# Last outputs formed in one VectorE operation, and the first key weights loaded in two quarters

## Chip, cores and metric

One core of a Trainium2 chip. The metric is the device time of one execution in microseconds (us), the median over runs. The span that a profile shows is some 1.8 us shorter than the device time of the same execution.

## Reference

A linear-attention block and a token-mixing MLP, both with a residual, in bf16:

```python
x = A_x                                            # [1, 2048, 1024]
h  = x + A(layernorm(x), wqkv, wo)                 # linear attention, phi(t) = elu(t) + 1
h2 = h + B(layernorm(h), w1, b1, w2, b2)           # mixer over the sequence, F = 3584
# B: u = gelu(h^T w1 + b1);  y = (u w2 + b2)^T
```

What matters for the change: at the start the first tiles of x are normalised, transposed and multiplied by the key columns of `wqkv`. At the end the last outputs are a matrix product plus `b2` plus the residual `h`.

## The kernel before

The head. `wkv` holds key and value weights; `hk` is half of the 8 row blocks. SP is the SyncE queue.

```python
xs = {0: load_x(0, True)}              # x tile 0, one half on SP's queue, one on ACT's
xs[1] = load_x(1)                      # SP
pin(nc.scalar.dma_start(wkv[:, 0:hk, 0:CW], wqkv_v[:, 0:hk, D:D + CW]))      # 512 KB, ACT's queue
nc.sync.dma_start(wkv[:, hk:ND, 0:CW], wqkv_v[:, hk:ND, D:D + CW])           # 512 KB, SP's queue
# ... cut: ACT's table load, x tile 2, more key weights, x tiles 3 to 5 ...
k_parts(0, 0, range(0, 6))             # PE: first six key matmuls, need row blocks 0 to 5
# ... cut ...
transpose_in(2)                        # PE transposes x tile 2, ACT copies it out of PSUM
ln_stats(3); stats(3)                  # fourth x tile: DVE statistics, ACT log and exp (rstd)
phi_dve((0, 0))
w_sums(kmov, slice(0, 1))              # DVE, a sum of weights, 1.2 us
norm_halves(3)                         # DVE normalises the fourth tile
# ... cut ...
transpose_in(3)                        # PE transposes it
```

The last quad. A quad is four 128-row output tiles, made by products with sums of weight blocks; there are four quads. For the last one the residual is fetched into SBUF (`self.hr`), so its outputs are stored plainly and not accumulated in DRAM.

```python
def out(self, sh, dh, a, b, op):
    # ... cut: choose ot, a piece of a dead weight buffer ...
    op(ot[:, a:b], b2_sb[:, i:i + 1])                                    # ACT (or DVE): PSUM + bias
    to = o_dram[i * P:(i + 1) * P, dh * CW + a:dh * CW + b]
    if (sh, dh) in self.hr:
        dve.tensor_tensor(ot[:, a:b], ot[:, a:b], self.hr[sh, dh][:, a:b], ALU.add)
        nc.sync.dma_start(to, ot[:, a:b])
    else:
        nc.gpsimd.dma_start(to, ot[:, a:b], accum_op=ALU.add)

def evac(self, sh, dh, ps, a=0, b=CW):
    self.out(sh, dh, a, b, lambda ot, bias: nc.scalar.activation(
        ot, ps[:, a:b], ACT.Identity, bias=bias, scale=1.0))
```

The very last product is cut into 384 and 128 columns, so that the first piece can leave while PE works on the second. In the middle, `load_w2(p, 0)` brings the next quad's even rows of `w2` (896 KB for each of two products) as soon as their buffer is free, and DVE's sums (`is`) read them.

## Time and profile before

Before: 559.9 us, median of three runs (559.51 to 560.59). The prediction below shows the lines of its profile. Four distances read from its trace:

| distance | before, us | how to read it |
|---|---|---|
| x tile 4 to transposes | 3.73 | from the first statistics of the fourth x tile (13.28) to PE's first transpose of it (17.01) |
| PE middle | 513.10 | from PE's 200th weight load to its 3380th, of 3387: nearly all work after the head |
| store lag | 1.42 | from the end of the 384 columns' matmuls (554.65) to the issue of the last store (556.07) |
| closing | 3.63 | from the end of the last matmul (555.04) to the end of the span (558.67) |

Matmul ends are modelled in such a trace, but in the same way in every kernel here.

### The profile page before, as it was taken

To read this page: it belongs to the slowest core of one execution; us is meant where nothing else is said; L and a number is where in the kernel's file an instruction comes from. 1 tells how busy PE (TensorE), PEld (TensorE's weight loads), DVE (VectorE), ACT (ScalarE), POOL (GpSimd) and SP (SyncE) were. 2 spreads that over 40 slices of the span, in tenths; PEclk is the share of its full clock that TensorE was granted. 3 is DMA by queue.
4 is the path that set the end of the run, shared out by engine and by line. 5 is a ranking of instruction groups with operands and counts; after the bars stand their busy time and mean duration, and the time that the engine had idled before them with its cause. 6 is when DMAs were issued, how large, how long until landed. Compare 5 with 4: busy or idle time off the path is not lost.

```text
span 558.7 us, 8921 instructions
## 1 busy us (share of the span) xinstructions
PE 550.3 (98%) x3370; PEld 320.7 (57%) x3387; DVE 442.7 (79%) x858; ACT 291.7 (52%) x619; POOL 26.2 (5%) x36
## 2 busy tenths in 40 slices
PE   7999999999999999999999999999999999999997
PEld 3444446645444444456766766666444667767665
DVE  6898888764579688889989889897996878749746
ACT  4747778676777877645455565464310312413312
POOL 1000000000000000000000000000003103103111
PEclk9999999999999999999999999999999999999999
DMA  9933332201956971202240431413769659849434
GB/s 306 298 76 76 76 76 39 39 0 47 340 151 176 325 208 75 76 0 74 80 151 0 151 122 31 150 38 96 197 209 237 190 127 244 212 133 238 93 106 74
DMA packets 83915, 74.51 MB, mean 133 GB/s; under 512 B 15634, under 2 KB 76320, under 8 KB 83872
## 3 DMA queue, kind: packets, MB, share of 16 engines
q1 hardware_dynamic: 79104, 69.61, 41.9%
q0 software_dynamic: 4096, 3.68, 4.8%
q10 hardware_dynamic: 672, 0.66, 0.4%
q8 instruction: 26, 0.43, 0.3%
q14 instruction: 17, 0.14, 0.1%
HBM read 59.12 MB, written 11.67 MB: 127 GB/s over the span
## 4 chain that ended last, share of the span: by engine, by line
PE 93%; DMA 2%; DVE 2%; ACT 1%; SPq 1%; issue 1%; DVEq 0%; ACTq 0%
PE psI L234 25%; PE psC L234 16%; PE acc_t L234 14%; PE psB L234 8%; PE psC L965 4%; PE psB L965 4%; PE psA L965 4%; PE psB L346 2%; PE psA L346 2%; PE acc_t L1295 2%; PE psE L965 2%; PE psC L346 2%; PE acc_t L887 2%; DMA x_sb<-in_A_x_dram 1%; PE psA L234 1%; PE kvps L916 1%
## 5 line engine op out<-in xcount | busy, mean ns | idle before, releaser
L234 PEld LDWEIGHTS <-is 128*128 128x128 f16 x736 | 71.8, 98 | 31.2 <-DVE hi L234 0.4
L234 PEld LDWEIGHTS <-sa 128*128 128x128 f16 x606 | 59.3, 98 | 27.1
L234 PEld LDWEIGHTS <-wq 128*128 128x128 bf16 (+1 forms) x496 | 48.4, 98 | 28.2 <-issue 1.0
L234 PE MATMUL acc_t<-wo_sb,pqT 128*128 128x512 f16 x256 | 55.6, 379 | 0.0
L492 POOL DMA_DIRECT2D out_dram<-wq x28 | 24.3, 927 | 520.3 <-DVE sa L338 401.3
L234 PEld LDWEIGHTS <-pqT 128*128 128x128 bf16 x256 | 24.9, 98 | 30.5 <-issue 0.6
L234 DVE TENSOR_TENSOR t<-psI,t 128x256 f32<-128x256 f32 (+1 forms) x45 | 20.8, 475 | 22.2 <-PE psI L234 20.9
L194 DVE TENSOR_SCALAR e_sb<-e_sb 128x512 bf16<-128x512 bf16 x64 | 18.4, 288 | 21.9 <-ACT e_sb L189 21.8
L234 PE MATMUL psC<-gs,wq 128*128 128x512 f16 x140 | 34.1, 379 | 0.0
L965 PEld LDWEIGHTS <-xs 128*128 128x128 f16 x208 | 20.1, 98 | 22.5 <-DVE xs L954 1.1
L234 PE MATMUL psC<-hT,sa 128*128 128x512 f16 x112 | 31.2, 379 | 0.0
L234 PE MATMUL psI<-hi,is 128*128 128x256 f16 x200 | 30.0, 273 | 0.0
L234 PE MATMUL psB<-hT,sa 128*128 128x512 f16 x112 | 29.7, 379 | 0.0
L234 PE MATMUL acc_t<-xnT,wq_sb 128*128 128x512 bf16 x125 | 29.3, 379 | 0.3
L189 ACT ACTIVATE e_sb<-acc_t 128x512 bf16<-128x512 f32 x32 | 19.1, 598 | 18.6 <-PE acc_t L1295 10.0
L234 DVE BATCH_NORM_STATS2 hst<-acc_t 128x6 f32<-128x512 f32 x32 | 21.4, 692 | 9.0 <-ACT h_bf L234 8.9
L965 PE MATMUL psA<-wkv,xnT 128*128 128x512 bf16 x98 | 26.2, 379 | 0.3
L965 PEld LDWEIGHTS <-xnT 128*128 128x128 bf16 x156 | 15.3, 98 | 18.0 <-issue 0.2
L234 PE MATMUL psC<-hT,wq 128*128 128x512 f16 x96 | 24.6, 379 | 0.0
L234 ACT CAST h_bf<-acc_t 128x512 bf16<-128x512 f32 x32 | 18.4, 581 | 11.9 <-PE acc_t L234 11.8
L234 DVE TENSOR_TENSOR e<-psI,es 128x256 f32<-128x256 f32 x20 | 8.5, 425 | 19.9 <-PE psI L234 17.8
L234 ACT COPY psI<-psI 128x256 f32<-128x256 f32 x50 | 18.0, 360 | 11.6 <-PE psI L234 9.7
(244 smaller groups left out, 1133.9 us busy)
## 6 DMA issues: line engine op xcount, KB each, us to landing
wq<-in_B_w_dram SPq DMA_DIRECT2D x14, 1024.0 KB, 7.9
wq<-in_B_w_dram SPq DMA_DIRECT2D x12, 896.0 KB, 7.4
gs<-parked SPq DMA_DIRECT2D x9, 896.0 KB, 4.7
shared_sb<-rd_dram SPq DMA_DIRECT2D x32, 128.0 KB, 3.8
out_dram<-h_bf SPq DMA_DIRECT2D x16, 256.0 KB, 2.0
x_sb<-in_A_x_dram SPq DMA_DIRECT2D x15, 256.0 KB, 3.0
w2o<-in_B_w_dram SPq DMA_DIRECT2D x4, 896.0 KB, 10.9
out_dram<-wq POOLq DMA_DIRECT2D x28, 128.0 KB, 5.0
```

Of the source, the lines that this page charges most:

```text
L189: pin(nc.scalar.activation(e_sb[:], src, ACT.Exp))
L194: pin(nc.vector.tensor_scalar(e_sb[:], e_sb[:], 1.0, PHI_EPS, ALU.min, ALU.add))
L234: return (lambda *a, **kw: pin(op(*a, **kw))) if self.always or getattr(Held, self.key) else op
L346: pe.matmul(ps[:, cols], lhsT=lhs[:, k, :], rhs=mv(k)[:, cols], start=(start and k == 0), stop=(k == self.nk - 1), skip_group_check=True,)
L492: nc.gpsimd.dma_start(to, ot[:, a:b], accum_op=ALU.add)
L887: mm = nc.tensor.matmul(pp[:, 0:CW], lhsT=xnT[:, kt, i * P:(i + 1) * P], rhs=wkv[:, kt, c * CW:(c + 1) * CW], start=(kt == 0), stop=(kt == ...
L916: pin(nc.tensor.matmul(kv_ps[b][:, sl, :], lhsT=pks[i % NPK][:, j * P:(j + 1) * P], rhs=vaugs[i % NVA][:, j, :], start=False, stop=(i == N ...
L965: pin(nc.tensor.matmul(ps[:], lhsT=lhs[:, k, :], rhs=rhs[:, k, :], start=(start and k == 0), stop=(k == hk2 - 1), skip_group_check=True,))
L1295: nc.tensor.matmul(qp[:, 0:SW], lhsT=wq_sb[:, kt, j * P:(j + 1) * P], rhs=xnT[:, kt, u * SW:(u + 1) * SW], start=(kt == 0), stop=(kt == ND ...
```

## The change

The intent: take ACT out of the last outputs, so that one DVE operation adds bias and residual to the PSUM value, and let the first key matmuls start when half of their weights are there. The diff, cut to its core:

```diff
-        def out(self, sh, dh, a, b, op):
+        def out(self, sh, dh, a, b, op, src):
             if (sh, dh) in self.hr:
-                ot = odd[self.p - 2][:, r:r + 2, :].rearrange("p a b -> p (a b)")
+                ot = odd[self.p - 2][:, r:r + 2, :].rearrange("p a b -> p (a b)")[:, a:b]
+                dve.scalar_tensor_tensor(ot, src, bias, self.hr[sh, dh][:, a:b], ALU.add, ALU.add)
+                hd.dma_start(to, ot)
             else:
-            op(ot[:, a:b], b2_sb[:, i:i + 1])
-            if (sh, dh) in self.hr:
-                dve.tensor_tensor(ot[:, a:b], ot[:, a:b], self.hr[sh, dh][:, a:b], ALU.add)
-                nc.sync.dma_start(to, ot[:, a:b])
-            else:
+                op(ot[:, a:b], bias)
                 nc.gpsimd.dma_start(to, ot[:, a:b], accum_op=ALU.add)
 ...
-            pin(nc.scalar.dma_start(wkv[:, 0:hk, 0:CW], wqkv_v[:, 0:hk, D:D + CW]))
+            for k in (0, hk // 2):
+                pin(nc.scalar.dma_start(wkv[:, k:k + hk // 2, 0:CW], wqkv_v[:, k:k + hk // 2, D:D + CW]))
```

(`evac` and `evac_shared` pass `src`, the PSUM columns or None for the sum in SBUF.)

More of the change, by code (lines that the diff above doesn't have):

```diff
@@ L476, in fetch @@
             self.hr[sh, dh] = t
-        def out(self, sh, dh, a, b, op):
+        def out(self, sh, dh, a, b, op, src):
             i = 2 * self.p + sh
+            to = o_dram[i * P:(i + 1) * P, dh * CW + a:dh * CW + b]
+            bias = b2_sb[:, i:i + 1]
             if (sh, dh) in self.hr:
                 r = 6 * dh + 2 + 2 * (a > 0)
-                ot = odd[self.p - 2][:, r:r + 2, :].rearrange("p a b -> p (a b)")
+                ot = odd[self.p - 2][:, r:r + 2, :].rearrange("p a b -> p (a b)")[:, a:b]
+                dve.scalar_tensor_tensor(ot, src, bias, self.hr[sh, dh][:, a:b], ALU.add, ALU.add)
+                hd.dma_start(to, ot)
             else:
@@ L485, in out @@
                 ots.append(ot)
-            op(ot[:, a:b], b2_sb[:, i:i + 1])
-            to = o_dram[i * P:(i + 1) * P, dh * CW + a:dh * CW + b]
-            if (sh, dh) in self.hr:
-                dve.tensor_tensor(ot[:, a:b], ot[:, a:b], self.hr[sh, dh][:, a:b], ALU.add)
-                nc.sync.dma_start(to, ot[:, a:b])
-            else:
+                op(ot[:, a:b], bias)
                 nc.gpsimd.dma_start(to, ot[:, a:b], accum_op=ALU.add)
@@ L495, in evac @@
             self.out(sh, dh, a, b, lambda ot, bias: nc.scalar.activation(
-                ot, ps[:, a:b], ACT.Identity, bias=bias, scale=1.0))
+                ot, ps[:, a:b], ACT.Identity, bias=bias, scale=1.0), ps[:, a:b])
         def evac_shared(self, sh, ps):
             self.out(sh, 1, 0, CW, lambda ot, bias: dve.scalar_tensor_tensor(
-                ot, ps[:], bias, self.e[:], ALU.add, ALU.add))
+                ot, ps[:], bias, self.e[:], ALU.add, ALU.add), None)
         def done(self):
```

## The prediction

> **What bounds the kernel now.** I read the page first: TensorE (PE) is busy for 550.3 of 558.7 us. Then the busy time by stage. The columns are the stretch, its length, then busy us and instructions of PE, weight load, VectorE (DVE), ScalarE (ACT) and POOL, then granted clock, DMA share and GB/s:
>
> ```profile
> 0.00:17.00 17.00, 13.53 (x70) 5.79 (x71) 11.40 (x43) 9.24 (x23) 1.89 (x8) 1.00 0.94 315
> 17.00:60.00 43.00, 42.49 (x223) 20.41 (x228) 37.84 (x82) 26.78 (x56) 0.00 (x0) 1.00 0.51 131
> 60.00:500.00 440.00, 439.21 (x2683) 256.38 (x2694) 352.60 (x664) 238.85 (x505) 13.90 (x16) 1.00 0.44 126
> 500.00:552.00 52.00, 52.00 (x377) 36.50 (x376) 38.80 (x65) 14.18 (x32) 10.45 (x12) 1.00 0.59 144
> 554.70:558.70 4.00, 0.34 (x7) 0.17 (x3) 0.88 (x3) 0.82 (x2) 0.00 (x0) 1.00 0.32 98
> ```
>
> From 17 us to 554.7 us PE has almost no hole (42.49 of 43.00, 439.21 of 440.00, 52.00 of 52.00) at full clock. So only the head, 17 us with 3.5 us of PE idle, and the tail, about 3.6 us after the last matmul, can give anything. The change touches exactly these two. What it can win is a few us at most, under 1% of 560.
>
> The head on PE, in order of time (start, length, what, idle before it and who ended it):
>
> ```profile
> 8.56 1.45 PE L887 MATMUL acc_t<-wkv,xnT 128*128 128x512 bf16 x6 [1.75 <-DMA wkv<-in_A_wqkv_dram]
> ...
> 14.63 1.89 PE L887 MATMUL acc_t<-wkv,xnT 128*128 128x512 bf16 x8
> 17.01 0.72 PE L1176 MATMUL tp<-ident,xn 128*128 128x128 bf16 x8 [0.49 <-DVE xn L866]
> ```
>
> The first line is the wait that the split is meant to shorten. The last is a second, later hole, which DVE ends. To see what sets that one I read the chain of waits in the head (start, length, what):
>
> ```profile
> 5.14 8.11 DMA x_sb<-in_A_x_dram
> ...
> 13.28 1.30 DVE st L856 x2
> ...
> 15.41 1.22 DVE shared_sb L939
> 16.63 0.34 DVE xn L866
> ...
> 17.01 0.72 PE tp L1176 x8
> ```
>
> The chain does not go through the key weights at all. It goes through the load of the fourth x tile, which lands at 13.26, then through DVE without a pause (statistics, a weight sum, the normalisation), then PE. Whatever PE does before 17.01, it waits there.
>
> The tail, from the same view:
>
> ```profile
> 552.00 2.66 PE psC L234 x14
> ...
> 554.69 0.59 ACT wq L495
> ...
> 555.30 0.36 DVE wq L234
> 555.66 0.14 DVEq L1833
> ```
>
> The last output columns are made by two operations in a row: ACT reads PSUM and adds the bias, DVE adds the residual in bf16. Then SyncE (SP) issues the stores. Its last two, in the timeline:
>
> ```profile
> 555.69 0.33 SPq L490 DMA_DIRECT2D out_dram<-wq  x1
> 556.07 0.43 SPq L490 DMA_DIRECT2D out_dram<-wq  x1
> ```
>
> The last landed at 557.63, and the end comes 1.04 us later, at 558.67.
>
> **What the Trainium skill says.** "Perfetto Trace Analysis", section Optimizing Scalar/DVE Operations: each operation has a fixed cost besides its elements (about 125 ns on DVE from PSUM) and some work can sit on either engine. The trace agrees on a fixed part: ACT takes 580 ns for 384 columns and still 359 for 128.
> "PSUM — Partial Sum Buffer", section Specifications: a VectorE instruction may take at most one tensor input from PSUM. The new operation has one (psC); bias and residual are in SBUF. The trace already holds this form, with one PSUM input and a per-partition bias, at 742 ns.
> "VectorE: DVE Perf Modes", section The perf-mode tier table: a two-tensor operation runs at two elements per cycle on bf16 in SBUF and at one with PSUM or fp32. The trace agrees: 425 ns for the old bf16 add of 512 columns, 742 for the form that reads PSUM. So the merged operation is slower than the DVE part that it replaces, and is a gain only because the ACT part before it goes.
> "DMA: Bandwidth & Descriptors", section Issuing engines are not separate DMA queues: transfers run on the same 16 DMA engines, whoever issues them. The head moves 315 GB/s at a DMA share of 0.94, so cutting a load in two adds no bandwidth; it can only let some of it be used sooner.
>
> **Part one, the final outputs.** Five outputs of the last quad change: two from a sum in SBUF, three from PSUM (512, 384 and 128 columns). Five ACT operations go, and five bf16 adds on DVE become five three-input operations. The built program confirms it: ACT loses five rows, DVE keeps its number and order, PE and the stores keep their order. The durations of what goes and what comes:
>
> ```profile
> L234 DVE SCALAR_TENSOR_TENSOR wq<-psC,b_sb,e 128x512 bf16<-128x512 f32 x6 | 4.5, 742 | 0.0
> ...
> L495 ACT ACTIVATE wq<-psC,b_sb 128x384 bf16<-128x384 f32 x1 | 0.6, 580 | 0.1
> L495 ACT ACTIVATE wq<-psC,b_sb 128x128 bf16<-128x128 f32 x1 | 0.4, 359 | 0.0
> ```
>
> Per column the three-input form costs about 1.04 ns (fp32 adds: 691 for 512, 420 for 256, so 271/256 = 1.06). Hence about 742 - 128 x 1.04 = 609 ns for 384 columns and 742 - 384 x 1.04 = 343 ns for 128. Now step through DVE; where two operations are both ready, the trace starts the second about 0.085 us before the first's end.
> Output 1: its sum is ready at 551.75; the operation runs 551.78 to 552.52 and is off the path.
> Output 2: sum ready at 553.30; 553.33 to 554.07.
> Output 3 (PSUM, 512): ready about 553.55, but DVE is taken; 553.99 to 554.73.
> Output 4 (PSUM, 384): its last matmul ends at 554.65, so as ACT did before it starts at 554.69, just as DVE comes free; to 555.30. Before, ACT and then DVE were done with it at 555.66.
> Output 5 (PSUM, 128): matmul done at 555.04; 555.21 to 555.56. Before: 555.80.
> The two last stores are 0.38 us apart in the trace (556.07 - 555.69): SP's own spacing, 0.33 issue plus 0.05. The fourth store follows its DVE operation by 0.03: 555.33. The fifth could start at 555.58 but waits for SP: 555.71 instead of 556.07. Gain 0.36 us on the path, set by the 384-column piece (580 + 359 and two hand-overs become 609 and one), not by the smallest. From issue to landing (1.56 us) and the closing 1.04 us do not change. There is perhaps 0.06 us more: SP ends with a fixed list of completion checks 0.06 apart, and as the split shifts the assignment of completion semaphores by one, the last store's stands one place nearer the end of the list.
> Sum of part one: 0.36 to 0.42 us.
>
> **Part two, the key weights.** The 512 KB on ACT's queue was issued at 1.18 and took 7.2 us: 8.4, and the first matmul began at 8.56. The x half before it on that queue landed at 0.74 + 2.7 = 3.4. If the weights arrive evenly between, the first quarter lands near (3.4 + 8.4)/2 = 5.9, my estimate. The first matmul then waits for ACT's copies of the transposed x (start 6.63, two in 0.65), so it moves to about 7.1. The third still needs the second quarter at 8.4, or up to 8.9 (1.67 + 7.2) if that now shares with SP's half. So two matmuls of 0.215 us move into the hole, and the group ends 0 to 0.43 us earlier than 10.0. All this lies before 17.01, where PE waits anyway: the second hole grows from 0.49 us to as much as 0.9. Bytes ahead of the fourth x tile are the same, so 13.26 stays. Worth on the path: 0. ACT's extra issue (0.45 us) delays its table load to about 2.1 to 3.4; its first operation is at 4.87, so that is free.
>
> **Sum.** 559.9 - 0.4 + 0 = 559.5 us.
>
> **Rivals.** (a) The split pays in full, because the fourth x tile is not what bounds the head. Then 0.43 us more: 559.1. For it: the wait removed is the longest of PE, 1.75. Against: the chain and the 0.49 hole at 17.01.
> (b) DVE becomes the bound of the tail: outputs 2 to 4 run on it back to back from 553.33, and at 50 ns more each than I reckon, the 384 piece starts late. That costs 0.1 to 0.15 of the 0.36: 559.7. For it: my margin at 554.69 is about 0.04 us.
> (c) The end does not follow the stores, because their landing is set by the DMA engines or by another queue. Then 559.9. Against: the last landing followed its issue by 1.56 and the DMA share is 0.32.
> (d) Two loads on ACT's queue push SP's loads, the fourth x tile among them, back by their issue time. Then up to 0.4 us later: 559.9 to 560.0. For it: every extra issue costs 0.4 to 0.5 us. Against: it is on ACT's sequencer, and SP's fourth tile is issued 8 us before it lands.
>
> **Range and chances.** The three runs before spread over 1.1 us, more than the gain, and the head hangs on when a DMA lands. So 558.9 to 560.2. No rival comes near 2% (11 us): chance of within 2% 0.99, the rest for a surprise either way.
>
> **What would show it.** Right: five ACT operations on the last outputs gone, DVE three-input operations of about 742, 609 and 343 ns, last store issued about 0.67 us after the last matmul instead of 1.03; first key matmul near 7.1, a hole before the third, and a hole ended by DVE at 17.0 that is larger than 0.49. Wrong: PE leaving that hole at another time than 17.0 (part two then acts through the x load), the 384 piece starting later than its matmul, or a new hole on PE between 17 and 554 us.

## The result, and the profile after

After: 560.12 us median of six runs (558.96 to 562.50), beside 559.70 for the kernel before in the same rounds. The ratio is 1.0008, with a 95% interval of 0.9985 to 1.0031: the same. A ratio here is the mean time of one kernel's runs over that of the other's of the same rounds, so it is not quite the ratio of the medians quoted. Executions over 1.5% slower than the fastest of the same kernel are left out of the means.

The tail moved as intended. The tail part of the chain of waits of the changed kernel (start, length, what):

```profile
552.33 2.31 PE psC L234 x12
554.64 0.43 issue
555.07 0.62 DVE wq L234
555.69 0.26 DVEq L1833
```

ACT is gone from it: PE, one DVE operation, then the closing. (The "issue" of 0.43 is read further down.) The groups of DVE instructions in the last 8 us have the mean ns of one as the number after the comma:

```profile
L234 DVE SCALAR_TENSOR_TENSOR wq<-psC,b_sb,wq 128x512 bf16<-128x512 f32 x1 | 0.7, 743 | 0.0
L234 DVE SCALAR_TENSOR_TENSOR wq<-psC,b_sb,wq 128x384 bf16<-128x384 f32 x1 | 0.6, 618 | 0.4 <-issue 0.4
...
L234 DVE SCALAR_TENSOR_TENSOR wq<-psC,b_sb,wq 128x128 bf16<-128x128 f32 x1 | 0.3, 342 | 0.0
```

The two last stores in the timeline, now one row of two issues, 555.72 and 556.10 in the trace:

```profile
555.72 0.81 SPq L234 DMA_DIRECT2D out_dram<-wq  x2
```

The last matmul ends at 555.37 here, so the last store leaves 0.73 us after it (before 556.07 - 555.04 = 1.03). The last stage by engine (same columns as in the prediction) shows ACT empty and DVE with two operations instead of three; the first line is the head:

```profile
0.00:17.00 17.00, 13.55 (x72) 5.72 (x73) 11.45 (x43) 9.13 (x23) 1.89 (x8) 1.00 0.91 307
...
554.70:558.70 4.00, 0.67 (x9) 0.43 (x7) 0.88 (x2) 0.00 (x0) 0.00 (x0) 0.87 0.31 98
```

In the head PE is busy for 13.55 us, as before (13.53). Its timeline says why the split brought nothing in this execution:

```profile
6.94 0.60 PE L886 MATMUL acc_t<-wkv,xnT 128*128 128x512 bf16 x2
9.10 1.02 PE L886 MATMUL acc_t<-wkv,xnT 128*128 128x512 bf16 x4 [1.56 <-DMA wkv<-in_A_wqkv_dram]
...
16.96 0.72 PE L1176 MATMUL tp<-ident,xn 128*128 128x128 bf16 x8 [0.33 <-DVE xn L865]
```

The wait for weights of 1.75 us became one of 1.56, moved behind the second matmul. The sixth key matmul starts at 9.75, before at 9.64.

So the tail gave 3.63 - 3.27 = 0.36 us. Yet the two spans are alike, 558.67 and 558.64, because PE's middle is 513.47 instead of 513.10. That 0.37 lies away from the edited lines, and the same kernel looked at again (after_again below) has 513.07: PE lost 0.15 near 156 us and 0.22 near 521 us. The experiments had three questions: is the tail's gain real and what fixed its size; what did the split do; and what takes time in the middle.

### The profile page after: what moved, and what is told of

Read it like the earlier page. It is cut to its first block, busy times and chain, and to the rows that moved or that the text cites. A ratio compares the mean times of both kernels' runs of the same rounds, so it can differ in the third digit from the quotient of the medians.

```text
span 558.6 us, 8933 instructions
## 1 busy us (share of the span) xinstructions
PE 551.3 (99%) x3387; PEld 320.3 (57%) x3387; DVE 444.0 (79%) x858; ACT 288.7 (52%) x614; POOL 26.3 (5%) x36
## 4 chain that ended last, share of the span: by engine, by line
PE 90%; DMA 5%; DVE 3%; ACT 1%; issue 1%; SPq 0%; DVEq 0%; ACTq 0%
PE psI L234 23%; PE psC L234 14%; PE acc_t L234 14%; PE psB L234 8%; PE psB L964 4%; PE psC L964 4%; PE psA L964 4%; PE psA L346 2%; PE acc_t L1295 2%; PE psB L346 2%; DMA x_sb<-in_A_x_dram 2%; PE psE L964 2%; PE psC L346 2%; DMA wq<-in_B_w_dram 2%; PE acc_t L886 2%; PE psA L234 1%
```

## The experiments

All distances, one profiled execution each. "w2 wait" is DVE's wait for the last quad's `w2` load between 500 and 530 us.

| kernel | span | weights landed | 6th key matmul | transposes of tile 4 | x tile 4 to transposes | PE middle | w2 wait | store lag | closing |
|---|---|---|---|---|---|---|---|---|---|
| before | 558.67 | 8.43 | 9.64 | 17.01 | 3.73 | 513.10 | 0 | 1.42 | 3.63 |
| after | 558.64 | 5.00, 9.06 | 9.75 | 16.96 | 3.73 | 513.47 | 0.2 | 1.12 | 3.27 |
| after_again | 558.28 | 5.18, 9.35 | 10.04 | 17.01 | 3.98 | 513.07 | 0 | 1.12 | 3.26 |
| tail_only | 558.90 | 6.39 | 8.44 | 16.04 | 3.73 | 514.59 | 1.3 | 1.12 | 3.34 |
| split_only | 558.38 | 5.25, 8.48 | 9.17 | 16.46 | 3.74 | 513.42 | 0 | 1.42 | 3.57 |
| head_order | 557.84 | 5.93 | 8.21 | 15.28 | 3.43 | 514.11 | 0.5 | 1.42 | 3.64 |
| head_order_split | 558.18 | 5.22, 8.21 | 8.90 | 15.62 | 3.73 | 514.18 | 1.0 | 1.42 | 3.56 |
| tail_seen | 561.09 | 8.49 | 10.22 | 18.35 | 4.05 | 514.53 | 1.0 | 1.07 | 3.28 |
| tail_double | 559.67 | 6.07 | 8.17 | 16.04 | 3.73 | 514.71 | 1.4 | 1.78 | 3.99 |
| w2_half | 557.22 | 5.99 | 8.19 | 15.64 | 3.73 | 513.01 | 0 | 1.42 | 3.64 |
| w2_half_head | 556.81 | 5.93 | 8.12 | 15.19 | 3.36 | 513.16 | 0 | 1.42 | 3.64 |
| best | 556.90 | 5.93 | 8.22 | 15.28 | 3.43 | 513.51 | 0.3 | 1.06 | 3.12 |
| split_again | 559.30 | 5.13, 8.72 | 9.40 | 16.66 | 3.73 | 514.13 | 0.7 | 1.42 | 3.58 |
| split_ahead | 557.84 | 5.07, 6.41 | 8.33 | 16.18 | 3.73 | 513.15 | 0 | 1.42 | 3.58 |

"Weights landed" is the 512 KB half, or its two quarters. Store lag of best is from its piece of 320 columns. The first four experiments, tail_only to head_order_split, went together, against 559.94 for the kernel before.

### One part alone

tail_only is the changed kernel with the load undivided:

```diff
-            for k in (0, hk // 2):
-                pin(nc.scalar.dma_start(wkv[:, k:k + hk // 2, 0:CW], wqkv_v[:, k:k + hk // 2, D:D + CW]))
+            pin(nc.scalar.dma_start(wkv[:, 0:hk, 0:CW], wqkv_v[:, 0:hk, D:D + CW]))
```

> The changed kernel with the key weights loaded in one piece again: the outputs part alone. My theory (the tail gain is real, 0.3 to 0.4 us, and hidden in the time by what scatters elsewhere): from the end of the last 384-column matmul to the issue of the last store about 1.12 us, as in the changed kernel, against 1.42 us in the kernel before; from the last matmul's end to the end of the span about 3.24 us against 3.63; first key matmul back at 8.5 us. Time 0.3 to 0.4 us below before, which 5 rounds with single runs scattered over more than 1 us may not resolve. Rival (the merged operations slow the tail or the end waits for something else): the distance from the last matmul to the end stays at 3.6 us or more.

Measured: 559.77 us, ratio 0.9991 (0.9978 to 1.0005). The store lag is 1.12, as with both parts, and the closing 3.34, where I had expected 3.24: the missing 0.06 went with the split. The first key matmul was not back at 8.5 us. It started at 7.35, for the undivided half landed at 6.39, two microseconds earlier than in the profile of before.

split_only is the kernel before with the opposite edit, two quarters and the old outputs.

> The kernel before with the key weights loaded in two quarters: the load part alone. My theory (worth nothing, since PE waits at 17 us for the fourth x tile whatever it did before): first key matmul near 6.9 to 7.1 us, third near 9.0, transposes of the fourth tile start within 0.1 us of the statistics of that tile plus 3.73 us, so near 17.0, and the distance from last matmul to end stays 3.63 us. Time equal to before. Rival (the split pays in full): the transposes of the fourth tile start near 16.6 and the time is 0.4 us lower. Second rival (the split costs): the fourth x tile lands later than 13.3 and all moves with it.

Measured: 560.18 us, ratio 1.0004 (0.9991 to 1.0016). The store lag stays at 1.42, but the closing is 3.57, 0.06 less than before. The fourth tile's transposes start at 16.46, as the first rival said, but not for its reason: the tile's statistics began at 12.72, and the transposes 3.74 after them, as the theory said. The third key matmul starts at 8.53 (expected near 9.0).

What follows: the merged operation alone brings the last store 0.30 us earlier and the end 0.29. The split alone brings the end 0.06 nearer to the last matmul, with the tail's operations untouched; three later kernels with the split and the old outputs repeat that (3.56 to 3.58). Both parts together: 0.365. So the tail's sum is additive, and no timing could show it: 0.37 of 560 us is 0.07%, and the narrowest interval of these runs is 0.12% to either side.

### A head with its operations reordered, without and with the split

To see whether the split pays once the head is less tight, I put the fourth tile's statistics ahead of ACT's copies of the third, and its normalisation ahead of the 1.2 us weight sum:

```diff
-            transpose_in(2)
+            tp2 = [transpose_half(2, h) for h in range(2)]
             ln_stats(3)
             stats(3)
+            for t in tp2:
+                pin(nc.scalar.copy(*t))
             phi_dve((0, 0))
-            w_sums(kmov, slice(0, 1))
             norm_halves(3)
+            w_sums(kmov, slice(0, 1))
```

> The kernel before, in which the head normalises the fourth x tile before the first weight sum on DVE, and computes its rstd on ACT before the copies of the third tile's transposes: this takes away the second hole on PE, the one at 17 us. My theory (that hole bounds the head): transposes of the fourth tile start near 16.4 us instead of 17.0, with no hole or one under 0.15 us before them, and the time falls by about 0.6 us, of which 5 rounds may show the sign. Rival (another wait takes its place at once): PE gets a new hole of about the same size between 16 and 25 us and the 200th weight load is not earlier than in the kernel before.

Measured: 560.16 us, ratio 0.9998 (0.9984 to 1.0011). The fourth tile's transposes start at 15.28 with no hole before them, but the expected 0.6 us does not show in the time.

> The same with the key weights in two quarters. With the second hole gone, PE's own progress from the first key matmul on sets the head, so the split can show itself. If the split helps the first group of matmuls, the transposes of the fourth tile start about 0.4 us earlier than without it. My theory after the profile of the changed kernel (the second quarter landed at 9.06, later than the undivided half at 8.43, so the group ended 0.1 us later in spite of its early start): they start 0 to 0.15 us later than without the split.

Measured: 559.95 us, ratio 0.9993 (0.9981 to 1.0005). The fourth tile was there at nearly the same time (first statistics at 11.89, without the split 11.84), but its transposes start at 15.62, 0.35 later (0 to 0.15 expected), again with no hole on PE just before. The waiting PE did at the third key matmul is then time lost. That is one pair of executions.

Head_order starts the transposes 1.74 us earlier than the kernel before. 0.97 of that stands in tail_only as well, with the operations in their old order: it comes from the late weights in the profile of before, not from the reordering. And the PE middle of head_order is 1.0 us longer: a good part of the lead is lost again before the end. tail_only loses 1.49, more than its lead. Weight loads of the same number, compared with the kernel before, show where: head_order loses 0.42 near 155 us and 0.60 between 508 and 521, tail_only 0.14 and 1.35. The waits of tail_only, first those of DVE and then those of PE, between 500 and 530 us (waiting operation, releaser, us in total, times, longest):

```profile
DVE is L234 <- DMA wq<-in_B_w_dram: 1.3, 1, 1.3
```

```profile
PE psI L234 <- DVE is L234: 0.8, 1, 0.8
```

DVE waits for the last quad's `w2`, and PE for DVE. The kernel before has neither line. In its trace that load landed 8.8 us after its issue, in tail_only 10.1.

### What bounds 500 to 530 us

w2_half loads only half of that quad's even rows. The result is wrong.

```diff
+        ks = slice(0, NFP // 2 if p >= NSP - 2 and not second else NFP)
         q.dma_start(
-            (odd[p] if second else even[p % 2]),
-            B_w2[...].rearrange(...)[:, :, second, :],
+            (odd[p] if second else even[p % 2])[:, ks, :],
+            B_w2[...].rearrange(...)[:, ks, second, :],
```

> The kernel before, but of the last quad's even w2 rows only the first half is loaded (the result is wrong on purpose; the rest of the buffer holds the rows of the quad before). Theory (between 512 and 524 us the path waits for that load to land, 8.8 to 10.1 us after its issue, and there a head that was early loses its lead): the load lands some 4 us earlier, no wait of PE or DVE is left in that stretch, and the distance from PE's 200th to its 3380th weight load is at most 513.1, about 512.8 to 513.1. Rival (the lead is lost on ACT at 155 us or spread over the run): the distance stays where the start of the fourth tile puts it, 513.1 for a late head and 514 or more for an early one.

> The same half load with the head's operations reordered (statistics of the fourth x tile ahead of the copies of the third). Theory (the last w2 load is what takes an early head's lead): the distance from PE's 200th to its 3380th weight load is within 0.3 us of that of the kernel with the half load alone, and the span is shorter by what the fourth tile's transposes start earlier, so of the two the one with the earlier transposes ends earlier by 0.8 to 1.2 times the difference. Rival (lost on ACT at 155 us and elsewhere): the distance is 0.7 us or more longer, as it was with the whole load (514.1 against 513.1).

w2_half_head adds the reordered head. Measured: 559.49 us, ratio 0.9992 (0.9961 to 1.0022), and 558.72 us, ratio 0.9965 (0.9939 to 0.9990), against 560.60 for the kernel before on that chip (its 11 runs include one of 564.62 at a clock of 0.994, which lifts their mean). The PE middle is 513.01 and 513.16, 0.15 apart, though both heads were early (15.64 and 15.19); the two lines of waits are gone in both. The transposes start 0.45 earlier in the second and its span is 0.41 shorter, 0.9 of it. So without that load's wait an early head reaches the end.

That an early head is what brings the wait about is not shown, and the traces speak against it. In all twelve with the whole load, the later of its two transfers is issued 2.14 us after PE's 3000th weight load, so an early head issues it early too. (In the two with half the rows it is issued 2.27 us before that weight load, so they change when it starts as well as its size.) What differs is the time from issue to landing, 8.75 to 10.23 us, and DVE's wait is in the order of that time: none up to 8.97, 0.2 at 9.01, 0.5 at 9.39, 1.0 at 9.81, 1.4 at 10.23. tail_seen has the latest head of all and waits 1.0; split_ahead, with its transposes at 16.18, does not wait. Why the load takes longer in one execution than in another stays open.

The rival, a loss near 155 us, is small where the rows are halved (none and 0.08) and in tail_only (0.14). In head_order it is 0.42 of the 1.0, and PE waits 0.5 us for ACT there; why only sometimes, no run tests.

In the table the six kernels with no w2 wait have a PE middle of 513.01 to 513.42, and the eight with one have 513.47 to 514.71, in the order of the wait but for ties.

### What fixes the tail's size

In the changed kernel the 384 columns' matmuls end at 554.98, but the operation starts at 555.07, 0.093 later; ACT had started 0.037 after. The trace has a separate wait instruction on DVE that ends at 555.029: the operation waits for three releasers (the residual's fetch, PE, and ACT). tail_seen lets DVE observe two of them earlier, with tail_only as its base:

```diff
                 hd.dma_start(to, ot)
+                if (sh, dh, b) == (1, 0, CW) and a == 0:
+                    seen = const.tile([P, 2], F32, name="seen")
+                    hs.copy(seen[:, 0:1], Mixer2.last.e[:, 0:1])                       # ACT
+                    dve.tensor_tensor(seen[:, 1:2], seen[:, 0:1], Mixer2.last.hr[1, 0][:, 0:1], ALU.add)
```

> The merged last outputs with the key weights in one piece, plus two one-column operations: ACT copies a column of the last quad's shared sum, and DVE adds it to a column of the last fetched residual, before the operation of 384 columns. So DVE has seen both the fetch and ACT by then, and that operation waits for PE alone. Theory (the 0.06 us missing from my 0.36 is a separate wait instruction on DVE, needed because three releasers are waited for): the 384 operation starts 0.04 us after its last matmul instead of 0.09, and the last store is issued 1.06 to 1.07 us after the end of the 384 columns' matmuls instead of 1.12. Rival (DVE's first read of PSUM after PE is simply slower than ACT's, or DVE is still held by the operation before): stays at 1.12.

Measured (one look, 562.86 us, in an execution with the clock at 0.997 and half-speed matmuls in the head, so only its tail is used): the operation starts 0.039 after its matmul, and the store lag is 1.068. In the timelines the idle time's releaser changes, first the changed kernel, then tail_seen:

```profile
555.07 0.88 DVE L234 SCALAR_TENSOR_TENSOR wq<-psC,b_sb,wq 128x384 bf16<-128x384 f32 x2 [0.43 <-issue]
```

```profile
557.46 0.88 DVE L234 SCALAR_TENSOR_TENSOR wq<-psC,b_sb,wq 128x384 bf16<-128x384 f32 x2 [0.31 <-PE psC L234]
```

"Issue" in the first is not work: it is where the wait instruction hid PE as the releaser.

tail_double, again on tail_only, does the operation of 384 columns twice:

```diff
+                if b < CW:
+                    dve.scalar_tensor_tensor(ot, src, bias, self.hr[sh, dh][:, a:b], ALU.add, ALU.add)
                 dve.scalar_tensor_tensor(ot, src, bias, self.hr[sh, dh][:, a:b], ALU.add, ALU.add)
```

> The merged last outputs with the key weights in one piece, where the operation of 384 columns is done twice (the same values are written again). Theory (DVE, two SP issues and the landing are one serial chain to the end): one more operation of 0.62 us less 0.085 of overlap, so the last store comes 1.12 + 0.53 = 1.65 us after the 384 columns' matmuls and the end 3.34 + 0.53 = 3.87 us after the last matmul. Rival (part of it hides behind SP's issues or behind the closing checks): under 0.4 of the 0.53 shows at the end.

Measured (one look, 561.46 us): store lag 1.777 and closing 3.992, both 0.655 more than in tail_only. My 0.53 was too small: the second operation started 0.035 after the first's end, not 0.085 before it, probably because it writes the same place (not tested). What was asked is answered: all of it reaches the end.

### The changed kernel again, and a version that uses what was learned

> The changed kernel once more, unaltered. Theory (its tail is fixed, its head and its stretch at 512 to 524 us hang on when two loads land): the last store comes again 1.12 us after the 384 columns' matmuls and the end 3.27 us after the last matmul, both to 0.03; the fourth tile's transposes again start 3.7 us after its first statistics (or later, if PE is still busy), wherever between 11.8 and 14.3 us that tile lands; the time is within 0.3% of the kernel before. Rival (the tail's gain was luck of one execution): the tail's distances differ by more than 0.05 from the first look.

Measured: 560.07 us, ratio 0.9998 (0.9984 to 1.0012) against 560.41. Store lag 1.122 and closing 3.262, to 0.005 as in the first look. This execution makes the cleanest pair with the profile of before: transposes at 17.01 in both, PE middle 513.07 and 513.10, closing 3.26 and 3.63, spans 558.28 and 558.67. With head and middle alike, nearly the whole difference (0.39) is the tail's (0.37).

But its fourth tile took 3.98, and landed at 12.74, half a microsecond before that of the kernel before (13.26), to start its transposes at the same time. Its chain of waits in the head:

```profile
1.68 7.67 DMA wkv<-in_A_wqkv_dram
9.35 0.04 issue
9.39 1.02 PE acc_t L886 x4
...
13.50 1.24 PE acc_t L886 x5
14.74 0.24 PE tp L1176 x4
...
15.01 1.07 ACT xnT L1186 x2
16.08 0.20 ACT lnv L861
...
16.30 0.21 ACT rstd L862
...
16.54 0.42 DVE xn L865
...
17.01 0.72 PE tp L1176 x8
```

Here the chain begins at the second quarter of the key weights, issued at 1.68. PE was late by it, so the third tile's transposes were late, so ACT's copies of them stood in front of the log and exp that the fourth tile's normalisation waits for.

best is tail_only with the reordered head and another cut of the last product:

```diff
-            ..., CW - P if 2 * u + 2 == NSP else None,
+            ..., CW - P - HW // 4 if 2 * u + 2 == NSP else None,     # 320 and 192 columns
```

> The merged last outputs, key weights in one piece, the last product cut in 320 and 192 columns instead of 384 and 128, and the head's operations reordered. Reckoned: the 320 columns' matmuls end 0.59 us before the last matmul, their operation starts 0.09 later and takes 0.55 (from 342 ns for 128 and 618 for 384 columns), so its store is issued 0.08 after the last matmul; the operation of 192 columns takes 0.41 and starts 0.04 after the last matmul, so the last store is issued 0.48 us after the last matmul, where it was 1.03 in the kernel before and 0.73 with the cut at 384. The end comes 3.34 - 0.25 = 3.09 us after the last matmul. The head's lead of about 1 us is partly lost at 512 to 524 us (the distance from PE's 200th to its 3380th weight load 513.5 to 514.3). Time 0.5 to 1.5 us below the kernel before, ratio 0.997 to 0.999; the interval may well not exclude 1. Rival (two stores close together collide at the end): the last store lands more than 1.65 us after its issue.

Measured: 558.86 us (558.20 to 559.37), ratio 0.9974 (0.9961 to 0.9986), some 1.5 us less than the kernel before, and the interval excludes 1. In its timeline:

```profile
553.29 0.94 DVE L234 SCALAR_TENSOR_TENSOR wq<-psC,b_sb,wq 128x320 bf16<-128x320 f32 x2 [0.25 <-PE psC L234]
```

```profile
553.87 0.81 SPq L234 DMA_DIRECT2D out_dram<-wq  x2
```

The last matmul ends at 553.77 and the last store is issued at 554.26, 0.48 after it as reckoned, and lands 1.59 later, so the two stores do not collide. Closing 3.12. Against the one profile of before the span is 1.78 shorter: 1.84 at the 200th weight load, 0.51 in the closing, and 0.58 given back in between (taken to the last matmul, since the 3380th weight load falls 0.17 earlier with the other cut). Of the 1.84, tail_only has 0.98 without the reordering, since its weights came in time.

### Why the second quarter is late

In all four executions with the split so far (the changed kernel twice, split_only, head_order_split) the second quarter landed at 8.21 to 9.35. The undivided half landed at 5.93 to 6.39 in six of eight, and at 8.43 and 8.49 in two, the kernel before's profile being one. In those two, 14 of the load's 16 completions were there at 6.05, and the last two came at 7.20 and 8.43, and at 7.83 and 8.49.

The Trainium skill, "DMA: Bandwidth & Descriptors", section Queues, rings and completion order, says that each DMA engine takes turns between the queues it has work for, a packet at a time. SP's half is issued at 1.66 and ACT's second quarter at 1.67, so they should land side by side. In the changed kernel they do, at 8.84 and 9.06; in the four executions they are 0.16 to 1.21 apart. split_ahead gives the second quarter to SP ahead of its half:

```diff
-            pin(nc.scalar.dma_start(wkv[:, 0:hk, 0:CW], ...))
+            pin(nc.scalar.dma_start(wkv[:, 0:hk // 2, 0:CW], ...))
+            nc.sync.dma_start(wkv[:, hk // 2:hk, 0:CW], ...)
             nc.sync.dma_start(wkv[:, hk:ND, 0:CW], ...)
```

> The kernel before with the key weights loaded in two quarters on ACT's queue, once more, for the same chip as the next run. Theory (the second quarter is issued at 1.68, just behind SP's half at 1.66, and so lands with that half and not before it): first quarter lands near 5.1, second quarter at 8.0 to 9.4 us, within 1 us of SP's half, and PE waits before the third key matmul, which starts at 8.3 or later; the sixth at 8.9 or later. Rival (the second quarter's late landing was chance in four executions): it lands before 7 and the sixth key matmul starts near 8.2, as it mostly does with the undivided load.

> The kernel before with the key weights in two quarters, where the second quarter is issued by SP ahead of SP's own half instead of by ACT after its first quarter. Theory (a transfer lands in the order in which it was issued among all queues): the second quarter lands at 6.0 to 6.6 us, before PE can use it, PE has no wait for weights of 0.3 us or more, and the sixth key matmul starts at 8.1 to 8.4 us. Rival (dividing the load is itself what costs): the second quarter lands at 7.5 or later and a hole before the third matmul stays.

split_again is split_only once more, on the same chip as split_ahead. Measured (one look each, 561.08 and 559.65 us): second quarter at 8.72 and at 6.41. PE's key matmuls, split_again and then split_ahead:

```profile
8.76 1.02 PE L887 MATMUL acc_t<-wkv,xnT 128*128 128x512 bf16 x4 [1.08 <-DMA wkv<-in_A_wqkv_dram]
```

```profile
7.05 1.66 PE L887 MATMUL acc_t<-wkv,xnT 128*128 128x512 bf16 x6
```

The hole before the third is gone (0.2 us remain before the fifth, which needs SP's half, landed at 8.07), and the sixth key matmul starts at 8.33. So it is not the dividing that makes the second quarter late. The quarter was issued at the same time in both, 1.67 and 1.66. What differs is that SP's half stands behind it in the same queue, issued at 2.13, and not beside it in another; queue and order were changed together, with one look each. Single late completions add to it: in split_again 11 of the quarter's 16 were there at 7.14 and the last came at 8.72, in split_ahead 15 at 5.82 and the last at 6.41. The sixth key matmul still starts no earlier than with most undivided loads (8.12 to 8.44): there the half lands before ACT's copies of the transposed x allow a first matmul at 7.0 to 7.4.

## Why the prediction was right or wrong

**The time.** 559.5 was predicted, 560.12 and 560.07 measured, the kernel before 559.70 and 560.41 beside them. The six runs of the changed kernel span 3.5 us, so medians inside the range are no proof of the 0.4. The reasons hold for the tail and only in part for the head.

**Part one, mechanism right.** ACT's five operations went, the durations were 743, 618 and 342 ns where 742, 609 and 343 were reckoned, the two stores stayed 0.38 apart, and tail_double shows that what is added to DVE's operation is added to the end. From 743 ns for 512 columns and 342 for 128 the slope is 1.04 ns per column and the rest 208 ns, of the order of twice the 125 ns that the Trainium skill ("Perfetto Trace Analysis", section Optimizing Scalar/DVE Operations) gives for DVE on PSUM; it says that profiled durations show about twice.

**Part one, the term that was mis-sized.** "Output 4 ... as ACT did before it starts at 554.69": the hand-over from PE was taken over at 0.04 and measured 0.093, because this operation, with its three releasers, has a wait instruction of its own. So the last store came 0.30 and not 0.36 earlier, 0.73 after the last matmul and not 0.67. tail_seen took that 0.055 back. The 0.06 that I gave as "perhaps", from the order of the closing checks, fits what came with the split in the four kernels that have the old outputs (0.054 to 0.077 less in the closing than the same head without it). I saw it as a distance; no run changed the order of the checks alone. Together 0.365, at the lower end of 0.36 to 0.42.

**Part two, the failed step: the wait read from one execution.** I took the 1.75 us hole in front of the first key matmul as a property of the kernel, and so the split as moving two matmuls into it. Six of the eight profiles with the load undivided have the weights before PE can use them. What I read was a load of whose 16 completions the last two came 1.1 and 2.4 us after the fourteenth. The first quarter landed at 5.00 to 5.25 (5.9 reckoned), and the first matmul did move to 6.94 and 7.11 (7.1 predicted). But the second quarter, reckoned at 8.4 to 8.9, came at 8.21 to 9.35, and against the usual undivided case the group ended later, not 0 to 0.43 earlier: its sixth matmul started at 8.90 to 10.04 with the split, at 8.12 to 8.44 without. The second hole, said to grow beyond 0.49, was 0.33 and 0.09 in the two looks at the changed kernel.

**"The chain does not go through the key weights at all"** was true of the profile I had and of three of the five executions with the split as changed. In after_again and head_order_split it goes through the second quarter, and the cost there was some 0.25 us (3.98 instead of 3.73) and 0.35. The times do not resolve it: split_only is 1.0004 with 1 well inside. So "worth 0" holds within what can be timed, and where it is not 0 it is a loss.

**The rivals.** (a), the split in full, failed. (b), DVE as the bound, failed: its operation of 512 columns ended at 554.64, 0.34 before the matmuls it had to wait for next. (c), an end that does not follow the stores, failed with tail_double. (d), SP's loads pushed back, came true, in another way than I gave. The chain of waits of the changed kernel, then that of tail_only:

```profile
0.74 2.90 DMA x_sb<-in_A_x_dram
...
3.66 0.38 SPq L1163
...
4.08 9.13 DMA x_sb<-in_A_x_dram
```

```profile
0.74 3.09 DMA x_sb<-in_A_x_dram
...
3.85 8.43 DMA x_sb<-in_A_x_dram
```

With the split, SP's last issue before the fourth tile reuses the completion semaphore of a half of the first x tile and waits for it to land (at 3.64); undivided, only the fourth tile's own issue waits (until 3.83). So with the split as changed that tile's load is issued at 4.08 to 4.27 (five executions), in the six with the undivided weights in time at 3.81 to 3.98. The tile lands at 11.86 to 13.21, four times of five at 12.70 or later, against 11.81 to 12.29. The profile of before hid this, since its tile was late too (issued at 5.14, landed at 13.26): "13.26 stays" was read from the same late execution.

What I had not named is the stretch at 500 to 530 us. I listed "a new hole on PE between 17 and 554" as a sign of being wrong; it came, without the change having a part in it: in tail_only and head_order as well, and not in after_again.

**Open.** Not settled are why single loads have one or two completions that come 2 us late, how much of the fourth tile's later landing comes from its later issue, and why the last `w2` load takes 8.75 us in one execution and 10.23 in another.

## What to carry to other kernels

Before shortening a wait that one profile shows, see whether it is there in a second execution: here the longest wait of the engine at the bound was a late load of that run, and the load divided to cure it came late in all five executions, where its second part was queued beside another queue's transfer. A gain far below the timing's spread can still be proved by a distance inside the trace (last matmul to end), with one part of the change at a time and one cost doubled. And before expecting an early stage to pay, look at what the middle does with the lead: here a load that is needed some 9 us after its issue and took 8.75 to 10.23 decided how much of it was kept.

## What the Trainium skill lacked or had wrong

- "Perfetto Trace Analysis", section Identifying Dependency Chains, says that wait instructions may be put ahead of an instruction that waits for several engines. It lacks their cost and their look: the operation started 0.093 us after its matmul with one and 0.039 without, and the profile showed the time as "issue" and not as a wait for PE.
- "DMA: Bandwidth & Descriptors", section Queues, rings and completion order: taking turns between queues fits the runs (8.84 and 9.06 us for two transfers issued 0.01 us apart on two queues; 6.41 and 8.07 when both went through one), though in another execution the two queues' transfers came 1.21 apart. The page does not say how unevenly the 16 completions of one 512 KB load can come; its section Latency and other measured facts says that DMA engines 7 and 15 are usually slower than the others, without a size. Here 14 were there at 6.05 us and the last two at 7.20 and 8.43, and only in two of eight executions was it like this; the traces kept do not number the engines, so whether it was those two is not known.
